# Spectral mixing and routed experts on one core: x read in runs of eight rows, tables and first weights on GpSimd's queue, two batches' copies on ScalarE

## The chip, the cores and the metric

The kernel runs on one core of a Trainium2 chip. The metric is the device time of one execution in microseconds. Before the change it is 1658.18 us, the median of three runs (1657.53 to 1659.67). A profile comes from one further execution of its own.

A core has TensorE (PE, with its weight loads as PEld), VectorE (DVE), ScalarE (ACT), GpSimd (POOL) and SyncE (SP), each with its own stream of instructions in program order. DMAs are issued from the streams of SP, ScalarE and GpSimd (SPq, ACTq and POOLq in the profile) and carried out by 16 DMA engines.

## The reference

```
X = rfft(x, axis=1)                       # x: (8, 2496, 256) float32
y = irfft(X * (filt_r + 1j*filt_i))       # one complex filter for each frequency and channel
x2 = y.reshape(19968, 256)
e = token_ids * 2654435761 % 8            # one of 8 experts for each token
out[e == k] = relu(x2[e == k] @ w1[k]) @ w2[k]     # w1: (8, 256, 1024), w2: (8, 1024, 256)
```

## The kernel before

**The transform.** The sequence length 2496 is split as 39 x 64: position = 64*n1 + n2, with n1 under 39 and n2 under 64. Each of the eight batches passes three stages, all made of float32 matmuls against tables.

- *Stage 1* is a transform over n1. To fill the partitions three values of n2 are stacked: a tile of x has 117 partitions (H = 3 groups of 39), and along its free side HN = 21 columns j of 256 channels. Group h holds n2 = 3j + h. The 64th value, n2 = 63, is left over: it stands as a 22nd column in group 0 alone. `load1` (L171 to L188) reads x in three loads of eight columns (XL), each as one DMA for every group, where a row of 256 channels (1 KB) is followed by the one three positions on; the left-over row has a DMA of its own (L187). `stage1` multiplies by `wf_t`, ScalarE copies the result from PSUM, and ScalarE's queue writes it to a buffer d1 in DRAM (L226), indexed by the place 3j + h.
- *Stage 2* is a transform over n2 with the filter and the way back. `load2` (L228) reads d1 with the 64 places on partitions, as five pieces of four frequencies (tiles t2). `forward` multiplies by `d_t` (L240); VectorE multiplies by the filter in four instructions (L246, L249 twice, L250); `back` (a step later) multiplies by `e_t`, the transposed `d_t` (L262); ScalarE copies (L265) and writes to d2 in DRAM (L269). There are eleven steps for a batch, of which ten have a forward half.
- *Stage 3* is the inverse transform over n1. `load4` (L281) reads d2, `stage3` multiplies by `wi_t`, VectorE copies the result into a tile o (L205, and L200 for the last two columns), beside which it writes each token's number (L287). Then one indirect DMA for each of the 22 columns (L298) scatters the rows to their slots in a buffer xs in DRAM; the slots come from `sidx`. There are two tiles o, and six pieces for a batch.

`products` (L190) is shared by stages 1 and 3 and takes the copying function as an argument.

**The routing.** `count` and `route` count the tokens of each expert and give each token a slot, so that the slots of a tile of 128 belong to one expert; `places` (L467) writes the slots to DRAM and reads them back as `sidx`, in the layout of stage 3. `tile_experts` and `experts` give each tile's expert (`chunk_i`). `blanks` scatters empty rows to unused slots.

**The experts.** A main loop over 163 tiles loads 128 rows of xs (L604), transposes them (`turn`, L612), multiplies by w1 (`up`, L623), applies the relu on ScalarE (L627) and VectorE (L629), multiplies by w2 (`down`, L635), copies (L638) and scatters to the output (L639). Weights are held for two tiles; SP reads an expert's number into a register and loads 1 MB each of w1 and w2 (L322, L324), skipped where the expert stays. The tiles come in four stages: those of a stage hold tokens of the first 2, 4, 6 or 8 batches alone. The two weight buffers serve first as room for x (batch 0 and the first third of batch 1).

**The order.** It is written out by hand. Each piece of work has a time, all are sorted by it, and each engine gets its instructions in that order (L567 to L587). Negative times are the prologue, ahead of the main loop: batches 0 and 1 entirely, batch 2 up to the start of stage 2, the routing and the tables. Pieces with times from 0 on are put into the main loop, one time unit for a tile. `load_tables` (L341) reads one part of `d_t` and of the two filters (four DMAs for these, two of which go backwards by rows); `spread_filters` copies them to the other 64 partitions, on VectorE and ScalarE; `way_back` makes `e_t` from `d_t` on TensorE. Part 0 serves the first four steps of stage 2 and part 1 the rest.

On SP the prologue's order is: x of batch 0; tables part 0; stage 2 input, piece 0 of batch 0; x of batch 1, first third; tables part 1; x, second third; piece 1; x, last third; pieces 2 to 4; `wi_t`; the weights of tiles 0 and 1; then the inputs of batch 1's stage 2, batch 0's stage 3 and x of batch 2, mixed.

Of the kernel before, what the change touches and what calls it, by code (L numbers as in the profile page):

```python
# [12 lines left out]
I32 = mybir.dt.int32  # L13
# [6 lines left out]
P = 128  # L20
# [4 lines left out]

N1, N2 = 39, 64
NS, NQ = N1 // 2 + 1, 64
H, HN = 3, 21  # L30
NR = H * N1
NK = 2 * H * NS
SG = 4
# [29 lines left out]


def dft_tables():
    n1, n2 = np.arange(N1), np.arange(N2)
    s, q = np.arange(NS), np.arange(NQ)
    ph = 2 * np.pi * np.outer(n1, s) / N1
    w = np.stack([np.cos(ph), -np.sin(ph)], 1)
    wf = np.zeros((H, N1, H, 2, NS))  # L70
    wi = np.zeros((H, 2, NS, H, N1))
    v = np.stack([2 * np.cos(ph), -2 * np.sin(ph)], 0)
    v[0, :, 0], v[1, :, 0] = 1.0, 0.0
    for h in range(H):
# [14 lines left out]
    f32 = np.float32  # L89
    return (wf.reshape(NR, NK).astype(f32), wi.reshape(NK, NR).astype(f32),  # L90
            d.reshape(P, NS, P).astype(f32))


def route_table():


    t = np.zeros((P, G + 2 + NQP + HN + 1), np.float32)
    p = np.arange(P)
    n1, j = np.arange(NR) % N1, np.arange(HN)
    t[:NR, G + 2 + NQP:-1] = (N2 * n1 + np.arange(NR) // N1)[:, None] + H * j  # L100
    t[:N1, -1] = N2 * np.arange(N1) + N2 - 1
# [9 lines left out]
def kernel(  # L111
# [38 lines left out]
    dps = pool(ctx, "dps", 1, PSUM)  # L150

    ident = keep.tile([P, P], F32)
    sidx = keep.tile([NR, B, N2], I32)
    tokno = keep.tile([NR, HN + 1], F32)
    chunk_i = keep.tile([1, 2, NT], I32)
    wf_t = cpool.tile([NR, NK], F32)
# [5 lines left out]
    class Batch:  # L162
# [8 lines left out]
        def load1(self, v):  # L171

            k = self.b * NV + v
            if k < 4:
                xt = ws[k // 2][k % 2][0:NR]
                if k % 2 == 0:
                    xt = xt.rearrange("p d (j c) -> p (d j) c", c=C)
            else:
                xt = xpool.tile([NR, XL, C], F32, name=f"x_{self.b}_{v}", tag="x")
            self.x[v] = xt  # L180
            off, n = x.offset + self.b * S * C, min(XL, HN - XL * v)
            for h in range(H):
                nc.sync.dma_start(out=xt[N1 * h:N1 * h + N1, 0:n, :],
                                  in_=bass.AP(tensor=x.tensor, offset=off + (H * XL * v + h) * C,
                                              ap=[[N2 * C, N1], [H * C, n], [1, C]]))
            if n < XL:
                nc.sync.dma_start(out=xt[0:N1, n, :],  # L187
                                  in_=bass.AP(tensor=x.tensor, offset=off + (N2 - 1) * C, ap=[[N2 * C, N1], [1, C]]))  # L188

        def products(self, w, rows, cols, src, dst, copy, u, name):  # L190

# [91 lines left out]
        def stage3(self, u):  # L283

            n = min(XG, HN + 1 - XG * u)
            o = opool.tile([NR, XG, W], F32, name=f"o_{self.b}_{u}", tag="o")
            nc.vector.tensor_scalar(o[:, 0:n, C:].bitcast(I32),  # L287
                                    tokno[:, XG * u:XG * u + n].unsqueeze(2).to_broadcast([NR, n, W - C]),
                                    float(self.b * S), None, op0=OP.add)
            v, half = divmod(u, XL // XG)  # L290
            self.products(wi_t, 2 * NS, N1, self.t4[v][:, half * XG:half * XG + XG, :], o, nc.vector.tensor_copy, u, "pd")
            for i in range(n):
                j = XG * u + i
                r, k = (NR, H * j) if j < HN else (N1, N2 - 1)
                scatter(o[0:r, i, :], sidx[0:r, self.b, k:k + 1], f"xs_{self.b}")

    def scatter(rows, index, group):
        st = nc.gpsimd.indirect_dma_start(  # L298
            out=xs[:], out_offset=bass.IndirectOffsetOnAxis(ap=index, axis=0),
            in_=rows, in_offset=None, bounds_check=NT * TB - 1, oob_is_err=False)  # L300
        for other in ["xs_pad", "xs_read"] + [f"xs_{b}" for b in range(B)]:
            tc.declare_no_dep(st.ins, group=other, reason="distinct rows")
        tc.add_to_no_dep_group(group, st.ins)
# [7 lines left out]
    def weights(i, which):  # L311

        if i >= NT:
            return
        if i >= 2 and which == 0:
            ws[i] = ws[i - 2]
        e = nc.sync.value_load(chunk_i[0:1, 0, i:i + 1], min_val=0, max_val=E - 1)
        kw = {}
        if i >= 2:
            kw = {"cond": nc.sync.value_load(chunk_i[0:1, 1, i:i + 1], min_val=0, max_val=1)}  # L320
        if which == 0:
            nc.sync.dma_start(out=ws[i][0][:], in_=moe_w1[bass.ds(e, 1)].rearrange("one (dp p) f -> p (one dp) f", p=P), **kw)  # L322
        else:
            nc.sync.dma_start(out=ws[i][1][:], in_=moe_w2[bass.ds(e, 1)].rearrange("one (fp p) d -> p (one fp) d", p=P), **kw)  # L324


    rctx = ctx.enter_context(ExitStack())
# [12 lines left out]

    def load_tables(part):  # L341
        sl = S_PARTS[part]
        nc.sync.dma_start(out=d_t[:, sl, :], in_=d_dram.ap()[:, sl, :])
        for k in range(2):
            load_filter(k, sl)

    def load_filter(k, sl):
        filt = (filt_r, filt_i)[k]
        for q in range(2):
            off, step = (0, C) if q == 0 else (N1 * C, -C)  # L350
            nc.sync.dma_start(
                out=f_t[k][32 * q:32 * q + 32, sl, :],
                in_=bass.AP(tensor=filt.tensor, offset=filt.offset + off + sl.start * step,
                            ap=[[N1 * C, 32], [step, sl.stop - sl.start], [1, C]]))
# [112 lines left out]
    def places():  # L467
        slot, slot_i = rv["eid"], rv["eid_i"]
        nc.vector.tensor_reduce(slot[:], rv["acc"][:].rearrange("p e j -> p j e"), axis=AX.X, op=OP.add)
        nc.vector.tensor_copy(slot_i[:], slot[:])  # L470
        nc.gpsimd.dma_start(out=slot_dram[:].rearrange("(p j) -> p j", p=P), in_=slot_i[:])
        for h in range(H):
            n = N2 if h == 0 else H * (HN - 1) + 1
            slots = slot_dram[:]
            nc.gpsimd.dma_start(out=sidx[N1 * h:N1 * h + N1, :, 0:n],
                                in_=bass.AP(tensor=slots.tensor, offset=slots.offset + h,
                                            ap=[[N2, N1], [S, B], [1, n]]))

    def tile_experts():
# [85 lines left out]


    todo = part1(0, spaced(-153, -143, NU)) + [(-152.5, count), (-152.4, route)]  # L567
    todo += [(-152.3, lambda: load_tables(0)), (-141, lambda: load_tables(1))]
    todo += [(t, lambda k=k: way_back(k)) for k, t in enumerate([-142.7, -142.5, -123.5, -123, -122.5])]
    todo += [(-129, lambda: spread_filters(0)), (-122.3, lambda: spread_filters(1)), (-129.5, places)]  # L570
    todo += part2(0, spaced(-128, -90.6, N_2), -142)
    todo += part1(1, spaced(-124, -99, NU), [-141.5, -140.5, -136])
    todo += [(-119, tile_experts), (-113, experts), (-108, blanks)]
    todo += [(-110, lambda: nc.sync.dma_start(out=wi_t[:], in_=wi_dram.ap()))]
    todo += [(-104 + 5 * i, lambda i=i: (weights(i, 0), weights(i, 1))) for i in range(2)]
    todo += part2(1, spaced(-90, -58, N_2), -97) + part3(0, spaced(-81, -48, NU), -90.5)
# [113 lines left out]
```

## Time and profile before

| what | value |
|---|---|
| median of three runs | 1658.18 us |
| profiled execution, its own time | 1654.79 us |
| its span, first to last instruction | 1653.1 us |
| mean granted TensorE clock | 0.963 |
| TensorE busy | 1521.8 us (92%) |
| TensorE weight loads busy | 1380.7 us (84%) |
| VectorE busy | 552.2 us (33%) |
| GpSimd busy | 349.1 us (21%) |
| ScalarE busy | 205.0 us (12%) |
| moved by DMA | 258.28 MB in 172156 packets, mean 156 GB/s |

A window row gives the stretch in us from the start of the span, its length, and for TensorE, its weight loads, VectorE, ScalarE and GpSimd the busy time in us with the count of instructions; then the granted TensorE clock, the DMA share (the mean busy share of the 16 DMA engines) and GB/s moved. A share can come out slightly above 1. A row of the waits gives who waited for whom: us in total, how many times, the longest. A timeline row gives start, duration, engine, line, operation, and count. The first instruction of the main loop's tiles is at 224.06 us.

### The profile page before, as it was taken

To read this page: it belongs to the slowest core of one execution; us is meant where nothing else is said; L and a number is where in the kernel's file an instruction comes from. 1 tells how busy PE (TensorE), PEld (TensorE's weight loads), DVE (VectorE), ACT (ScalarE), POOL (GpSimd) and SP (SyncE) were. 2 spreads that over 40 slices of the span, in tenths; PEclk is the share of its full clock that TensorE was granted. 3 is DMA by queue.
4 is the path that set the end of the run, shared out by engine and by line. 5 is a ranking of instruction groups with operands and counts; after the bars stand their busy time and mean duration, and the time that the engine had idled before them with its cause. 6 is when DMAs were issued, how large, how long until landed. Compare 5 with 4: busy or idle time off the path is not lost.

```text
span 1653.1 us, 26640 instructions
## 1 busy us (share of the span) xinstructions
PE 1521.8 (92%) x9522; PEld 1380.7 (84%) x9522; DVE 552.2 (33%) x1046; ACT 205.0 (12%) x347; POOL 349.1 (21%) x361
## 2 busy tenths in 40 slices
PE   4555669999999999999999999999999999999998
PEld 3434458888888999899989999999899999999997
DVE  6356243353243444324433433222211112121121
ACT  2211102111111111111110111000000000000000
POOL 0015500240331032212221223232211111111111
PEclk7788789999999999999999999999999999999999
DMA  8999666866785796396726844453244312222220
GB/s 205 205 272 265 188 143 173 239 179 161 209 221 156 248 256 163 105 246 149 222 79 186 243 119 145 124 155 116 82 146 138 112 64 92 89 83 90 89 81 12
DMA packets 172156, 258.28 MB, mean 156 GB/s; under 512 B 16297, under 2 KB 141660, under 8 KB 171897
## 3 DMA queue, kind: packets, MB, share of 16 engines
q1 hardware_dynamic: 125057, 170.95, 38.2%
q10 hardware_dynamic: 27608, 42.13, 9.0%
q0 software_dynamic: 19360, 43.50, 8.0%
q8 instruction: 76, 1.25, 0.3%
q14 instruction: 55, 0.45, 0.1%
HBM read 431.38 MB, written 86.09 MB: 313 GB/s over the span
## 4 chain that ended last, share of the span: by engine, by line
PE 43%; issue 37%; POOL 7%; DMA 6%; DVE 4%; SPq 1%; POOLq 1%; ACT 1%; ACTq 0%; DVEq 0%
PE ups L623 15%; PE dps L635 15%; POOL out_dram L639 5%; PE pa L203 4%; PE pd L203 3%; PE pb L240 3%; PE pc L262 3%; DMA t<-d 2%; DVE z L249 2%; POOL xs L298 2%; DMA d<-t 1%; DMA w<-in_x_dram 1%; DMA d<-g 1%; PE xps L612 1%; DVE y L246 1%
## 5 line engine op out<-in xcount | busy, mean ns | idle before, releaser
L623 PEld LDWEIGHTS ups<-xt,w 128*128 128x128 f32 x5216 | 609.5, 192 | 9.7 <-DVE xt L614 1.0
L623 PE MATMUL ups<-xt,w 128*128 128x128 f32 x5216 | 610.5, 275 | 0.6 <-DVE xt L614 0.6
L635 PE MATMUL dps<-w,ht 128*128 128x256 f32 x2608 | 595.9, 382 | 0.0
L635 PEld LDWEIGHTS dps<-w,ht 128*128 128x128 f32 x2608 | 492.5, 192 | 66.6 <-issue 1.6
L639 POOL DMA_INDIRECT out_dram<-osb,xg x163 | 159.9, 981 | 952.9 <-DVE osb L638 903.7
L629 DVE TENSOR_SCALAR ht<-ups 128x512 f32<-128x512 f32 x163 | 112.7, 691 | 535.8 <-PE ups L623 464.8
L298 POOL DMA_INDIRECT xs<-o,sidx x176 | 176.8, 1005 | 260.4 <-DVE o L205 191.8
L627 ACT ACTIVATE ht<-ups 128x512 f32<-128x512 f32 x163 | 97.4, 597 | 1026.4 <-PE ups L623 817.8
L638 DVE COPY osb<-dps 128x256 f32<-128x256 f32 x163 | 69.2, 424 | 405.0 <-PE dps L635 378.1
L240 PE MATMUL pb<-t,d_t 128*128 128x256 f32 x320 | 89.2, 406 | 43.4 <-DMA t<-d 43.4
L249 DVE TENSOR_TENSOR z<-pb,filt 64x512 f32<-64x512 f32 x160 | 110.2, 688 | 2.2
L262 PE MATMUL pc<-y,e_t 128*128 128x256 f32 x320 | 85.9, 392 | 26.6 <-DVE y L250 24.9
L240 PEld LDWEIGHTS pb<-t,d_t 128*128 128x128 f32 x320 | 62.2, 204 | 55.2 <-issue 46.4
L262 PEld LDWEIGHTS pc<-y,e_t 128*128 128x128 f32 x320 | 59.9, 193 | 43.2 <-issue 23.6
L203 PE MATMUL pd<-t,wi_t 120*117 120x256 f32 x320 | 81.9, 401 | 12.2 <-DMA t<-d 8.0
L246 DVE TENSOR_TENSOR y<-pb,filt 128x512 f32<-128x512 f32 x80 | 55.2, 689 | 74.5 <-PE pb L240 67.6
L203 PEld LDWEIGHTS pd<-t,wi_t 120*117 120x117 f32 x320 | 59.1, 191 | 25.1 <-issue 9.5
L265 ACT COPY g<-pc 128x512 f32<-128x512 f32 x80 | 46.9, 586 | 254.3 <-PE pc L262 226.9
L614 DVE COPY xt<-xps 128x256 f32<-128x256 f32 x163 | 67.4, 414 | 5.5 <-PE xps L612 5.5
L612 PE MATMUL xps<-ident,xg 128*128 128x128 f32 x326 | 62.5, 274 | 6.3 <-DMA xg<-xs 6.3
L203 PE MATMUL pa<-x,wf_t 117*120 117x256 f32 x264 | 64.8, 390 | 1.5 <-DVE z L249 1.5
L205 ACT COPY t<-pa 120x512 f32<-120x512 f32 x80 | 46.1, 587 | 123.3 <-PE pa L203 106.8
(93 smaller groups left out, 348.5 us busy)
## 6 DMA issues: line engine op xcount, KB each, us to landing
w<-in_moe_w_dram SPq DMA_DIRECT2D x326, 1024.0 KB
xg<-xs SPq DMA_DIRECT2D x163, 136.0 KB
t<-d SPq DMA_DIRECT2D x80, 256.0 KB
d<-g ACTq DMA_DIRECT2D x80, 256.0 KB
d<-t ACTq DMA_DIRECT2D x16, 960.0 KB
t<-d SPq DMA_DIRECT2D x16, 960.0 KB
x<-in_x_dram SPq DMA_DIRECT2D x39, 312.0 KB
d<-t ACTq DMA_DIRECT2D x8, 600.0 KB
```

Source lines behind the costliest of these rows:

```text
L203: nc.tensor.matmul(out=ps[0:cols * H, k, :], lhsT=w[:], rhs=src[:, 2 * i + k, :], start=True, stop=True)
L240: nc.tensor.matmul(out=ps[:, i, :], lhsT=d_t[:, s, :], rhs=self.t2[s // SG][:, s % SG, :], start=True, stop=True)
L246: nc.vector.tensor_tensor(out=y[:], in0=ps[:], in1=f_t[0][:, sl, :], op=OP.mult)
L249: nc.vector.tensor_tensor(out=z[b], in0=ps[a], in1=f_t[1][a, sl, :], op=OP.mult)
L262: nc.tensor.matmul(out=ps[:, i, :], lhsT=e_t[:, 2 * u + i, :], rhs=pr[:, i, :], start=True, stop=True)
L298: st = nc.gpsimd.indirect_dma_start(out=xs[:], out_offset=bass.IndirectOffsetOnAxis(ap=index, axis=0), in_=rows, in_offset=None, bounds_ch ...
L612: nc.tensor.transpose(out=ps[:, dp, :], in_=xg[i][:, dp * P:(dp + 1) * P], identity=ident[:])
L623: nc.tensor.matmul(out=ps[:, k, :], lhsT=w1[:, dp, fp * P:(fp + 1) * P], rhs=xt[i][:, dp, :], start=(dp == 0), stop=(dp == DP - 1))
L627: nc.scalar.activation(out=dst, in_=ps[:], func=AF.Relu)
L629: nc.vector.tensor_scalar_max(dst, ps[:], 0.0)
L635: nc.tensor.matmul(out=ps[:], lhsT=ht[:, fp, :], rhs=w2[:, fp, :], start=(fp == 0), stop=(fp == FP - 1))
L639: st = nc.gpsimd.indirect_dma_start(out=out[:], out_offset=bass.IndirectOffsetOnAxis(ap=xg[i][:, C:C + 1].bitcast(I32), axis=0), in_=o[:], ...
```

## The change

**x.** Group h now holds 21 neighbouring values of n2: group 1 has 0 to 20, group 2 has 21 to 41 and group 0 has 42 to 63, the left-over one included (`H0`). So eight columns of a partition are eight neighbouring rows of x, 8 KB in a run, and group 0's DMA is one row longer where a batch ends, instead of a DMA of its own. The places in d1 and d2 stay 3j + h; the order of n2 along them is a permutation, which `dft_tables` puts into `d_t`. `sidx` and the token numbers follow: `sidx` holds 22 slots for each partition and batch in place of 64.

**Queues.** The tables (`d_t`, filters) and the weights of tiles 0 and 1 are issued by GpSimd instead of SP. Part 0 of the tables goes first of all pieces; part 1 is issued inside `places`, between the write of the slots and the reads of `sidx`.

**Copies.** Stage 3 of batches 0 and 1 copies from PSUM on ScalarE instead of VectorE. The token numbers (L287) stay on VectorE.

**Times.** The prologue's times are new. On SP the order becomes: x of batch 0; piece 0; x of batch 1, first third; piece 1; x, second and last third; pieces 2 to 4; `wi_t`; and then as before, with the first two loads of x of batch 2 one place earlier each. Stage 1 of batch 1 ends ahead of step 7 of stage 2 of batch 0 (before: ahead of step 8), and `way_back` of part 1 and the spreading of part 1's filters stand around step 3 (before: ahead of step 2). The main loop's times are unchanged.

```diff
+H0 = (2 * HN, 0, HN)
...
 def dft_tables():
-    n1, n2 = np.arange(N1), np.arange(N2)
+    n1 = np.arange(N1)
+    n2 = np.array([H0[i % H] + i // H for i in range(N2)])
...
-    sidx = keep.tile([NR, B, N2], I32)
+    sidx = keep.tile([NR, B, HN + 1], I32)
...
-            off, n = x.offset + self.b * S * C, min(XL, HN - XL * v)
             for h in range(H):
+                n = min(XL, HN + (h == 0) - XL * v)
                 nc.sync.dma_start(out=xt[N1 * h:N1 * h + N1, 0:n, :],
-                                  in_=bass.AP(tensor=x.tensor, offset=off + (H * XL * v + h) * C,
-                                              ap=[[N2 * C, N1], [H * C, n], [1, C]]))
-            if n < XL:
-                nc.sync.dma_start(out=xt[0:N1, n, :],
-                                  in_=bass.AP(tensor=x.tensor, offset=off + (N2 - 1) * C, ap=[[N2 * C, N1], [1, C]]))
+                                  in_=bass.AP(tensor=x.tensor, offset=x.offset + (self.b * S + H0[h] + XL * v) * C,
+                                              ap=[[N2 * C, N1], [C, n], [1, C]]))
...
-            self.products(wi_t, 2 * NS, N1, self.t4[v][:, half * XG:half * XG + XG, :], o, nc.vector.tensor_copy, u, "pd")
+            copy = nc.scalar.copy if self.b < 2 else nc.vector.tensor_copy
+            self.products(wi_t, 2 * NS, N1, self.t4[v][:, half * XG:half * XG + XG, :], o, copy, u, "pd")
...
-                r, k = (NR, H * j) if j < HN else (N1, N2 - 1)
-                scatter(o[0:r, i, :], sidx[0:r, self.b, k:k + 1], f"xs_{self.b}")
+                r = NR if j < HN else N1
+                scatter(o[0:r, i, :], sidx[0:r, self.b, j:j + 1], f"xs_{self.b}")
...
-        e = nc.sync.value_load(chunk_i[0:1, 0, i:i + 1], min_val=0, max_val=E - 1)
-        kw = {}
+        eng, kw = nc.gpsimd if i < 2 else nc.sync, {}
+        e = eng.value_load(chunk_i[0:1, 0, i:i + 1], min_val=0, max_val=E - 1)
...
-            nc.sync.dma_start(out=ws[i][0][:], in_=moe_w1[bass.ds(e, 1)].rearrange("one (dp p) f -> p (one dp) f", p=P), **kw)
+            eng.dma_start(out=ws[i][0][:], in_=moe_w1[bass.ds(e, 1)].rearrange("one (dp p) f -> p (one dp) f", p=P), **kw)
...
-        nc.sync.dma_start(out=d_t[:, sl, :], in_=d_dram.ap()[:, sl, :])
+        nc.gpsimd.dma_start(out=d_t[:, sl, :], in_=d_dram.ap()[:, sl, :])
...
         nc.gpsimd.dma_start(out=slot_dram[:].rearrange("(p j) -> p j", p=P), in_=slot_i[:])
+        load_tables(1)
         for h in range(H):
-            n = N2 if h == 0 else H * (HN - 1) + 1
+            n = HN + (h == 0)
...
-    todo += [(-152.3, lambda: load_tables(0)), (-141, lambda: load_tables(1))]
-    todo += [(t, lambda k=k: way_back(k)) for k, t in enumerate([-142.7, -142.5, -123.5, -123, -122.5])]
-    todo += [(-129, lambda: spread_filters(0)), (-122.3, lambda: spread_filters(1)), (-129.5, places)]
-    todo += part2(0, spaced(-128, -90.6, N_2), -142)
-    todo += part1(1, spaced(-124, -99, NU), [-141.5, -140.5, -136])
-    todo += [(-119, tile_experts), (-113, experts), (-108, blanks)]
+    todo += [(-154, lambda: load_tables(0)), (-129.5, places)]
+    todo += [(t, lambda k=k: way_back(k)) for k, t in enumerate([-142.7, -142.5, -119.5, -119, -118.5])]
+    todo += [(-129, lambda: spread_filters(0)), (-118.3, lambda: spread_filters(1))]
+    todo += part2(0, spaced(-128, -95, N_2), -142)
+    todo += part1(1, spaced(-123.5, -105, NU), [-141.5, -135, -134.5])
+    todo += [(-117, tile_experts), (-113, experts), (-108, blanks)]
     todo += [(-110, lambda: nc.sync.dma_start(out=wi_t[:], in_=wi_dram.ap()))]
-    todo += [(-104 + 5 * i, lambda i=i: (weights(i, 0), weights(i, 1))) for i in range(2)]
-    todo += part2(1, spaced(-90, -58, N_2), -97) + part3(0, spaced(-81, -48, NU), -90.5)
-    todo += part3(1, spaced(-52, -20, NU), -60) + part1(2, spaced(-50, -18, NU), [-75, -70, -40])
+    todo += [(-107 + i, lambda i=i: (weights(i, 0), weights(i, 1))) for i in range(2)]
+    todo += part2(1, spaced(-94, -60, N_2), -103) + part3(0, spaced(-84, -51, NU), -94.5)
+    todo += part3(1, spaced(-54, -21, NU), -62) + part1(2, spaced(-52, -19, NU), [-85, -80, -41])
```

The filters' DMAs and that of w2 change their engine in the same way as those of `d_t` and w1.

More of the change, by code (lines that the diff above doesn't have):

```diff
@@ L98, in route_table @@
     p = np.arange(P)
-    n1, j = np.arange(NR) % N1, np.arange(HN)
-    t[:NR, G + 2 + NQP:-1] = (N2 * n1 + np.arange(NR) // N1)[:, None] + H * j
-    t[:N1, -1] = N2 * np.arange(N1) + N2 - 1
+    r = np.arange(NR)
+    t[:NR, G + 2 + NQP:] = (N2 * (r % N1) + np.array(H0)[r // N1])[:, None] + np.arange(HN + 1)
     for g, b in enumerate(STAGES):
@@ L316, in weights @@
             ws[i] = ws[i - 2]
-        e = nc.sync.value_load(chunk_i[0:1, 0, i:i + 1], min_val=0, max_val=E - 1)
-        kw = {}
+        eng, kw = nc.gpsimd if i < 2 else nc.sync, {}
+        e = eng.value_load(chunk_i[0:1, 0, i:i + 1], min_val=0, max_val=E - 1)
         if i >= 2:
-            kw = {"cond": nc.sync.value_load(chunk_i[0:1, 1, i:i + 1], min_val=0, max_val=1)}
+            kw = {"cond": eng.value_load(chunk_i[0:1, 1, i:i + 1], min_val=0, max_val=1)}
         if which == 0:
-            nc.sync.dma_start(out=ws[i][0][:], in_=moe_w1[bass.ds(e, 1)].rearrange("one (dp p) f -> p (one dp) f", p=P), **kw)
+            eng.dma_start(out=ws[i][0][:], in_=moe_w1[bass.ds(e, 1)].rearrange("one (dp p) f -> p (one dp) f", p=P), **kw)
         else:
-            nc.sync.dma_start(out=ws[i][1][:], in_=moe_w2[bass.ds(e, 1)].rearrange("one (fp p) d -> p (one fp) d", p=P), **kw)
+            eng.dma_start(out=ws[i][1][:], in_=moe_w2[bass.ds(e, 1)].rearrange("one (fp p) d -> p (one fp) d", p=P), **kw)
     rctx = ctx.enter_context(ExitStack())
@@ L350, in load_filter @@
             off, step = (0, C) if q == 0 else (N1 * C, -C)
-            nc.sync.dma_start(
+            nc.gpsimd.dma_start(
                 out=f_t[k][32 * q:32 * q + 32, sl, :],
@@ L471, in places @@
         nc.gpsimd.dma_start(out=slot_dram[:].rearrange("(p j) -> p j", p=P), in_=slot_i[:])
+        load_tables(1)
         for h in range(H):
-            n = N2 if h == 0 else H * (HN - 1) + 1
+            n = HN + (h == 0)
             slots = slot_dram[:]
             nc.gpsimd.dma_start(out=sidx[N1 * h:N1 * h + N1, :, 0:n],
-                                in_=bass.AP(tensor=slots.tensor, offset=slots.offset + h,
+                                in_=bass.AP(tensor=slots.tensor, offset=slots.offset + H0[h],
                                             ap=[[N2, N1], [S, B], [1, n]]))
```

## The prediction

> **What bounds the kernel now.** I read the 40 slices first, then the busy times of stretches, then who waited for whom, then the DMA view.
>
> ```profile
> PE   4555669999999999999999999999999999999998
> DMA  8999666866785796396726844453244312222220
> ```
>
> Each digit is a fortieth of the span, 41.3 us. TensorE is full from the sixth slice on; before that it is half idle while the DMA engines are full. The windows view puts figures to it (busy us per engine, clock, DMA share, GB/s):
>
> ```profile
> 0.00:157.00 157.00, 86.03 (x320) 64.22 (x320) 95.87 (x191) 33.42 (x52) 32.15 (x41) 0.83 0.93 238
> 157.00:225.00 68.00, 34.32 (x110) 24.38 (x110) 17.41 (x32) 7.67 (x14) 25.03 (x26) 0.68 0.78 198
> 225.00:1653.00 1428.00, 1401.43 (x9092) 1292.10 (x9092) 438.91 (x825) 163.95 (x281) 291.95 (x295) 0.99 0.51 145
> ```
>
> From 225 us, where the first expert tile runs, TensorE is busy 1401 of 1428 us, with the same work after the change. Its waits there come to 19.4 us, all on copies by VectorE and ScalarE and none on a DMA. So only the 225 us ahead of it can shrink, the prologue with 120.3 us of TensorE work in it. TensorE's waits in it are:
>
> ```profile
> PE pb L240 <- DMA t<-d: 43.4, 4, 14.3
> PE pc L262 <- DVE y L250: 17.6, 12, 2.3
> PE pa L203 <- DMA w<-in_x_dram: 11.2, 2, 10.1
> PE pd L203 <- DMA t<-d: 8.0, 1, 8.0
> PE xps L612 <- DMA xg<-xs: 6.3, 1, 6.3
> ```
>
> Columns: total us, times, longest. 69 us end on DMAs, 18 us on VectorE's filter product. The four waits for stage 2's input (28.4 to 37.9, 51.7 to 66.0, 102.6 to 112.6, 199.2 to 208.7) are the core of it. The longest is a matter of SP's order:
>
> ```profile
> 35.78 0.68 SPq L343 DMA_DIRECT2D d_t<-d_tbl  x1
> 36.50 1.22 SPq L351 DMA_DIRECT2D filt<-in_filt_r_dram  x2
> 37.76 1.85 SPq L351 DMA_DIRECT2D filt<-in_filt_i_dram  x2
> 40.37 8.85 SPq L183 DMA_DIRECT2D x<-in_x_dram  x3
> 49.26 2.98 SPq L232 DMA_DIRECT2D t<-d  x2
> ```
>
> The second piece of stage 2's input (L232 at 49.26) stands behind the second tables and two loads of x, and takes 14.3 us to land.
>
> **Part by part.** *x in 8 KB runs.* The DMA view of 5 to 10 us, where x is alone, and of 95 to 103 us, with weights and writes (slice lines left out):
>
> ```profile
> DMA packets 867, 0.86 MB, mean 171 GB/s; under 512 B 31, under 2 KB 867, under 8 KB 867
> q1 hardware_dynamic: 867, 0.86, 90.9%
> ...
> DMA packets 1883, 3.22 MB, mean 403 GB/s; under 512 B 135, under 2 KB 1432, under 8 KB 1883
> ```
>
> x in 1 KB packets moves 171 GB/s at a share of 0.91, so 188 GB/s with the engines full; the other stretch moves 403 at 1.05, so 384. The mean of the first 157 us is 238/0.93 = 256. No row has x in 8 KB runs, so its rate lies between 188 (no gain) and 384; I take 256, what the prologue's mixture reaches. Before 157 us x costs 2 x 2.56 + 2 x 0.96 = 7.0 MB: 37.2 us at 188, 27.3 at 256, 18.2 at 384. Gain **10 us** of DMA time (0 to 19). The eight small extra loads (L187, 0.32 us of issue each) also go. The Trainium skill ("DMA: Bandwidth & Descriptors", section "Specifications") gives 512 B as the smallest transfer at line rate. By that rule 1 KB packets have nothing to gain, this term would be 0 and my sum 13 instead of 23; the 171 GB/s beside 403 speak against the rule here.
>
> *Tables on GpSimd's queue.* 1.3 MB of d_t and 2.6 MB of filters leave SP. In 0 to 157 us SP's queue moved 23.14 MB in 63.0% of 157 us, 234 GB/s, and GpSimd's 3.51 MB in 7.3%, 306 GB/s: 3.9 MB take 12.8 us instead of 16.8, **4 us** (0 to 8, the upper end if the 4.2 MB of weights gain as well). On POOL each DMA is one instruction: 1.06 us for the slots, 0.69 for a sidx load of 312 runs, so ten table DMAs cost 7 to 11 us of an engine that is idle from 2.0 to 35.9. The first five go out at 2 us instead of 12 to 26; beside x they can delay the first x (landed at 10.06) or come in its gaps: -2 to +3 us on stage 2's start, which I take at +2. It cannot be more: VectorE's routing chain ends at 35.5 and the filter copy at 36.8, where the first product now starts at 40.0. The second five follow the write of the slots at 36, as on SP now, and stand ahead of the sidx loads; those have to be there by the first scatter (127.2), so their delay of some 5 us is hidden.
>
> *Order on SP.* Stage 2's second input is moved ahead of x's second third, and the tables are out of the way; it should land near 42. Steps two and three of stage 2 then no longer wait for it until 66. What is late next is the second half of the filters: it lands at 58.3 now and ScalarE negates it until 61.0. If that stays, the fifth step (product at 77.7 now) can start at 61: 16.7 us (5 to 22, by how much the tables suffer beside x). The remaining six steps need 6 x 2.77 = 16.6 us of VectorE and 3 us of routing, 20 us where 23.6 are spent: 3 us. The gap of 10.0 us at 102.6 to 112.6 ends on stage 2 input of the second batch, whose write was slowed by 4 MB of weights; after the change its stage 1 ends a step earlier and the weights are issued behind it: 7 us (0 to 10).
>
> *Copies of stage 3 on ScalarE.* For the first batch, interleaved with stage 2 of the second, VectorE is busy 35.5 us of 44 (113 to 157). It loses ten copies of 0.688 us and two of 0.42, 7.7 us, and ScalarE, busy 5.9 of those 44, gets them at 0.587: 7 us (0 to 7.7). If a copy waits on ScalarE for a free o tile (two tiles, 17.3 us of such waits on VectorE's L287 now), the copies of stages 1 and 2 and the writes ScalarE issues stand behind it.
>
> *First weights on POOL.* They stand behind seven scatters of blanks (9 us) and wait for chunk_i; behind them are the scatters of batch 0. They cost four instructions of 1 to 2.3 us (1024 runs at the sidx load's 2.2 ns), hidden by POOL's idle 29 us ahead of 127.2. SP loses 4.4 us of waiting for chunk_i ahead of stage 2's loads; inside the gap above.
>
> **The sum.** The chain of waits would give 16.7 + 3 + 7 + 7 = 34 us by 157 us, but the same 37.4 MB must pass. DMA is busy 0.93 x 157 = 146 us and idle 11; 10 + 4 us less busy leaves 132. With its idle time kept the stretch shrinks by 14, with none left by 25. I take 14 plus half of the idle, **20 us**; the DMA bound thus takes back 14 of the 34. After 157 us the third batch's stage 3 copies are paced by POOL: 22 scatters at 1.295 us are 28.5 of the 30.6 us from 167.9 to 198.5; 1 us at most comes from ScalarE. The last wait, for xg (215.3 to 224), has 0.96 MB of x ahead of it: 5.1 us at 188, 3.7 at 256, some 1.5 us. I take **3 us** for both (-4 to +4). Sum 23 us. The profiled execution took 1654.79 us (span 1653.1), 3.4 below the median of the runs, 1658.18; from the median: **1635 us**.
>
> On the queues the Trainium skill ("DMA: Bandwidth & Descriptors", section "Issuing engines are not separate DMA queues") says that issuing from several engines saves only issue time, as all share 16 DMA engines. By it the table term is 0 instead of 4 and the forecast 1639; the 306 against 234 GB/s above are rates of different packets and do not settle it.
>
> **Rivals.** *x is no faster in long runs.* For it: 12 KB packets of the second tables run beside x in 40 to 52 us, and that stretch reaches only 199 GB/s at 1.07. Then 0 + 4 + 5.5 by 157 us, and 1 behind: 10 us, **1648**. *DMA isn't the bound* and packets only look long because queues interleave: 403 GB/s in one stretch speaks for it, a share over 0.9 from 0 to 157 against it. Then the chain's 34 and 3: **1621**. *Slower: weights ahead of the scatters.* They share POOL's queue, and stage 3 has two o tiles, so the third waits until the weights have landed. If they are issued as late as now (93 us) and get a third of 256 GB/s, 4.2 MB take 49 us and land at 142; then come 42 scatters at 1.295 (54.4), the 6.7 us between batches and the 26.8 from the last scatter to the first tile: 230 instead of 225.3, **1663**. It decides once they land after 137.4; against it speak the earlier stages. *No change*: the main loop gives back what the prologue gains, since its order is fixed; its full TensorE speaks against it: **1658**.
>
> **How the numbers follow.** Forecast 0.46, x no faster 0.18, chain 0.20, no change 0.06, slower 0.10. A measurement of this kernel tells 0.2% (3.3 us) from no change; so faster is 0.84, same 0.06, slower 0.10. The range, 1618 to 1652, spans the second and third cases with their spread and leaves out the last two.
>
> **What would show it.** The first expert tile at about 202 us instead of 225; all later work the same. Packets under 8 KB fall by 17,000 to 20,000 and x's early rate rises over 220 GB/s. The wait of 14.3 us ahead of L240 is gone, and the filter's second half (L359) is what the fifth step waits for. VectorE's share in the overlap falls under 0.75 or the stretch is shorter. Wrong I would be if x stays near 171 GB/s, if the first scatter starts after 125 us, or if TensorE begins to wait for DMAs in the main loop.

## The result and the profile after

The changed kernel takes 1668.83 us (median of four runs, 1668.52 to 1671.55), the kernel before 1658.93 us on the same chip: a ratio of 1.0062, 95% interval 1.0045 to 1.0080. It is 10 us slower where 23 us faster was forecast. The profiled execution took 1668.82 us, its span is 1667.2 us.

The slices of the changed kernel, now 41.7 us each:

```profile
PE   3656559998999999999999999999999999999997
DMA  7988755756786796395726844443244312222220
```

TensorE is full from the sixth or seventh slice on, as before. The DMA row is no longer full ahead of that: 8, 7, 5 and 5 stand where 9, 6, 6 and 6 stood. The same three stretches in the windows view (us, then busy us of TensorE, weight loads, VectorE, ScalarE, GpSimd, then clock, DMA share, GB/s):

```profile
0.00:157.00 157.00, 84.26 (x304) 62.59 (x304) 87.08 (x175) 36.83 (x59) 34.51 (x49) 0.80 0.87 224
157.00:225.00 68.00, 33.54 (x112) 23.00 (x112) 5.81 (x15) 15.34 (x30) 31.09 (x32) 0.75 0.72 194
...
225.00:1667.00 1442.00, 1403.15 (x9106) 1292.36 (x9106) 444.87 (x834) 165.12 (x283) 292.48 (x295) 0.99 0.50 145
```

DMA engines are less busy by 157 us (0.87 for 0.93), as forecast, but they moved less too: 224 GB/s for 238. The saved busy time became idle time, not speed. TensorE's waits ahead of the main loop:

```profile
PE pb L239 <- DMA t<-d: 29.5, 5, 10.0
PE pd L202 <- DMA t<-d: 23.2, 2, 16.0
PE pa L202 <- DMA w<-in_x_dram: 20.8, 3, 13.7
PE pc L261 <- DVE y L249: 13.2, 9, 3.5
PE pd L197 <- issue: 8.6, 2, 5.2
```

The waits for stage 2's input fell from 43.4 to 29.5 us. Those for stage 3's input rose from 8.0 to 23.2, those for x of batch 0 from 11.2 to 20.8. In landmarks of TensorE's timelines (us from the start of the span):

| first matmul of | before | after |
|---|---|---|
| stage 1, batch 0 | 10.1 | 13.7 |
| stage 2, batch 0 | 37.9 | 42.9 |
| its third step (second input) | 66.0 | 60.2 |
| its fifth step | 76.6 | 78.6 |
| stage 2, batch 1 | 112.6 | 104.5 |
| stage 3, batch 0 | 124.7 | 131.5 |
| stage 3, batch 1 | 164.9 | 173.6 |
| first expert tile | 224.1 | 234.7 |

So the loss has two places: 5 us by the start of stage 2, of which 2 are left at its fifth step; and, after 8 us were won by the start of batch 1's stage 2, a swing of 15 us up to stage 3 of batch 0. From there the lead of the kernel before grows from 6.8 to 10.6 us. The rest of the two profiles' 14.1 us lies in the main loop (1429.0 and 1432.5 us). That is within the noise: in the profiles of set 2 below the main loop takes 1428.4 us before the change and 1424.2 after it.

The second place in POOL's and SP's timelines of the changed kernel (start, duration, engine, line, operation):

```profile
104.52 0.98 POOL L299 DMA_INDIRECT xs<-tok,at_i  x1 [0.30 <-issue]
105.48 0.78 POOL L323 DMA_DIRECT2D w<-in_moe_w_dram  x1
106.25 0.95 POOL L325 DMA_DIRECT2D w<-in_moe_w_dram  x1
107.18 0.73 POOL L323 DMA_DIRECT2D w<-in_moe_w_dram  x1
107.88 0.93 POOL L325 DMA_DIRECT2D w<-in_moe_w_dram  x1
134.44 1.06 POOL L299 DMA_INDIRECT xs<-o,sidx  x1 [25.64 <-ACT o L204]
```

and in its chain of waits (start, duration, what):

```profile
114.13 17.21 DMA t<-d
131.34 0.14 issue
131.47 3.73 PE pd L202 x8
```

The weights go out behind the last scatter of blanks, at 105 to 109 us (before: 83 to 93). The first third of stage 3's input, issued at 114.1 by SP, takes 17.2 us to land and TensorE waits 16.0 us for it. The DMA view of 112 to 132 us says with what it shared the engines (queue: packets, MB, share of 16 engines):

```profile
q1 hardware_dynamic: 1528, 1.90, 48.6%
q0 software_dynamic: 904, 3.44, 47.4%
q10 hardware_dynamic: 180, 0.58, 7.2%
```

GpSimd's queue (q0), in which nothing but the weights is left then, moved 3.44 MB, SP's (q1) 1.90. The first four microseconds of it, 114 to 118 us, show how the input fared right after its issue:

```profile
q0 software_dynamic: 379, 1.47, 100.2%
q10 hardware_dynamic: 10, 0.04, 2.5%
q1 hardware_dynamic: 1, 0.00, 0.1%
```

SP's queue moved nothing in them. In 118 to 122 us it moved 0.24 MB beside 0.89 MB of weights, and only from 122 us on, as the weights ran out, the bulk of what it had to move.

### The profile page after: what moved, and what is told of

Its sections match the earlier page's. It is cut to its first block, busy times and chain, and to the rows that moved or that the text cites. A ratio compares the mean times of both kernels' runs of the same rounds, so it can differ in the third digit from the quotient of the medians.

```text
span 1667.2 us, 26682 instructions
## 1 busy us (share of the span) xinstructions
PE 1521.0 (91%) x9522; PEld 1377.9 (83%) x9522; DVE 537.8 (32%) x1022; ACT 217.3 (13%) x371; POOL 358.1 (21%) x375
## 4 chain that ended last, share of the span: by engine, by line
PE 49%; issue 32%; DMA 9%; POOL 5%; DVE 3%; ACT 1%; SPq 1%; POOLq 0%; another core or an unknown queue 0%; ACTq 0%; DVEq 0%
PE ups L625 18%; PE dps L637 18%; POOL out_dram L641 4%; PE pd L202 3%; DMA t<-d 3%; PE pa L202 3%; PE pb L239 2%; PE pc L261 2%; DMA d<-t 2%; DMA d<-g 1%; POOL xs L299 1%; PE xps L614 1%; DVE z L248 1%; DMA w<-in_x_dram 1%; DMA xg<-xs 1%
## 5 line engine op out<-in xcount | busy, mean ns | idle before, releaser
L239 PE MATMUL pb<-t,d_t 128*128 128x256 f32 x320 | 90.6, 411 | 29.9 <-DMA t<-d 29.5
L202 PE MATMUL pd<-t,wi_t 120*117 120x256 f32 x320 | 82.0, 402 | 23.8 <-DMA t<-d 23.2
L202 PEld LDWEIGHTS pa<-x,wf_t 117*120 117x120 f32 x264 | 47.7, 186 | 15.0 <-ACT t L204 3.6
```

The costliest lines, as they stand in the source:

```text
L202: nc.tensor.matmul(out=ps[0:cols * H, k, :], lhsT=w[:], rhs=src[:, 2 * i + k, :], start=True, stop=True)
L239: nc.tensor.matmul(out=ps[:, i, :], lhsT=d_t[:, s, :], rhs=self.t2[s // SG][:, s % SG, :], start=True, stop=True)
```

## The experiments

Each set ran on one chip, with runs of the kernel before beside it; the sets ran on four chips (4 and 5 on one), and the kernel before took 1646 to 1657 us there. Ratios are to the kernel before of the same set, with 95% intervals. Runs of one kernel differ by 5 to 16 us within a set, so a single profile shows where a wait stands, and the ratio what it costs.

**Set 1: one part of the change undone.** The first weights on SP at their old times:

```diff
-        eng, kw = nc.gpsimd if i < 2 else nc.sync, {}
-        e = eng.value_load(chunk_i[0:1, 0, i:i + 1], min_val=0, max_val=E - 1)
+        e = nc.sync.value_load(chunk_i[0:1, 0, i:i + 1], min_val=0, max_val=E - 1)
+        kw = {}
...
-    todo += [(-107 + i, lambda i=i: (weights(i, 0), weights(i, 1))) for i in range(2)]
+    todo += [(-104 + 5 * i, lambda i=i: (weights(i, 0), weights(i, 1))) for i in range(2)]
```

> The changed kernel with the first weights issued by SP again, at their old times. Theory 'the weights collide': in the changed kernel GpSimd issues them at 105.5 to 108.8 us, behind the blanks, and their 4.2 MB share the DMA engines with batch 0's stage 3 input, for which TensorE waits 16.0 us until 131.5. On SP they go out once chunk_i is there (87 us in the changed kernel), so that wait falls under 6 us and the time falls by 8 to 11 us, to 1658 to 1661. Rival 'tables crowd x': the loss comes from the first 38 us, so 1667 to 1669 stays.

Measured 1.0057 (1.0035 to 1.0078).

Part 0 of the tables on SP, behind x of batch 0 (part 1 stays on GpSimd; the filters' DMAs follow `teng` as well):

```diff
-        nc.gpsimd.dma_start(out=d_t[:, sl, :], in_=d_dram.ap()[:, sl, :])
+        teng = nc.sync if part == 0 else nc.gpsimd
+        teng.dma_start(out=d_t[:, sl, :], in_=d_dram.ap()[:, sl, :])
...
-    todo += [(-154, lambda: load_tables(0)), (-129.5, places)]
+    todo += [(-152.3, lambda: load_tables(0)), (-129.5, places)]
```

> The changed kernel with part 0 of the tables on SP again, behind the x of batch 0 (part 1 stays on GpSimd). Rival 'tables crowd x': x's first third lands at 10 us instead of 13.7 and stage 2 starts at 38 instead of 42.9; if that carries through, the time falls by 5 us to 1664. Theory 'the weights collide': the early 5 us are absorbed further on (stage 2 of batch 0 ended only 2 us later than before the change), so the time falls by 0 to 2 us, 1667 to 1669.

Measured 1.0052 (1.0031 to 1.0074).

Stage 3's copies on VectorE:

```diff
-            copy = nc.scalar.copy if self.b < 2 else nc.vector.tensor_copy
+            copy = nc.vector.tensor_copy
```

> The changed kernel with stage 3's copies of batches 0 and 1 on VectorE again. Theory 'the weights collide': the copies were never what stage 3 waited for, because from 131 us on stage 3 is paced by GpSimd's scatters; 1667 to 1671. Rival 'ScalarE is the new bottleneck': copies waiting for a free o tile hold up those of stages 1 and 2 behind them on ScalarE (3.2 and 2.3 us of such waits in the changed kernel's last 40 us); undone, the time falls by 3 to 6 us, 1663 to 1666. If the copies were worth the 7 us that the prediction gave them, it rises to 1675.

Measured 1.0086 (1.0058 to 1.0114).

x in 1 KB runs again (the parts of the diff that touch n2, `sidx` and `load1` undone):

> The changed kernel with x read in 1 KB runs again (old grouping of n2, with the left-over row's own DMA), all else changed. Theory 'x is no faster in long runs': 13 to 14 GB/s for each DMA engine in the changed kernel's packets of x as against 12 to 13 in the old ones, so the time stays within 3 us of 1668.8. If the packing does what the prediction took (10 us of DMA time), the time rises by 5 to 10 us to 1674 to 1679. If long packets hold up the others' short ones, it falls by 3 us or more.

Measured 1.0096 (1.0064 to 1.0128).

The expectations were in us of another chip, and the set had no run of the changed kernel itself. That kernel has 1.0062 (1.0045 to 1.0080) in the result above and 1.0081 (1.0050 to 1.0112) in set 2, and all four intervals here overlap both. So no part taken back alone is shown to return anything. The theory that the weights on SP give back the whole loss is refuted: in that run's profile the waits for stage 3's input are down to 7.7 us from 23.2, and the time is still 1.0057. Nor does part 0 of the tables alone carry it.

**Set 2: the changed kernel as reference, and single parts put into the kernel before.**

> The changed kernel as it is, on the chip of this set, as the reference for its parts. All theories: 1.004 to 1.010 of the time before; TensorE's wait for batch 0's stage 3 input at 12 us or more.

> The kernel before as it is, for its profile on the chip of this set: ratio 0.998 to 1.002; first expert tile 8 to 12 us earlier than in the changed kernel's profile.

Measured 1.0081 (1.0050 to 1.0112) and 1.0010 (0.9987 to 1.0033). The first expert tile starts at 228.4 and 218.0 us in their profiles, and TensorE waits 12.2 us at the longest for stage 3's input.

The weights alone moved to GpSimd (the four lines of `weights` in the change's diff, at the old times):

> The kernel before with only the first weights moved to GpSimd, at their old times. They stand behind the seven scatters of blanks there (88 to 98 us) and go out at about 98 to 102 instead of 83 to 93. Theory 'the weights collide': they meet the inputs of batch 1's stage 2 and of batch 0's stage 3; slower by 4 to 10 us (1.0025 to 1.006). Rival 'tables crowd x': no effect of the weights, within 2 us (0.999 to 1.001).

Measured 1.0083 (1.0053 to 1.0112): this part alone costs as much as the whole change. Its POOL timeline:

```profile
100.37 0.97 POOL L298 DMA_INDIRECT xs<-tok,at_i  x1 [0.30 <-issue]
101.33 0.78 POOL L322 DMA_DIRECT2D w<-in_moe_w_dram  x1
102.10 0.97 POOL L324 DMA_DIRECT2D w<-in_moe_w_dram  x1
103.04 0.73 POOL L322 DMA_DIRECT2D w<-in_moe_w_dram  x1
103.73 0.93 POOL L324 DMA_DIRECT2D w<-in_moe_w_dram  x1
```

SP issued the same four at 83 to 87 us in the kernel before on this chip. TensorE waits for stage 3's input twice, 16.5 us in total, instead of once for 8.4. The write ahead of batch 0's input takes 10.6 us here, and the first third of that input 16.7 us to land.

The grouping of n2 alone (x in 8 KB runs):

> The kernel before with only the new grouping of n2, so that x is read in runs of 8 KB, at the old times. Prediction: 10 us of DMA time less, so 5 to 10 us faster (0.994 to 0.997). Theory 'x is no faster in long runs': within 3 us (0.998 to 1.002), with x alone (5 to 10 us) near 190 GB/s instead of 171.

Measured 1.0015 (0.9999 to 1.0031). The DMA view of 5 to 10 us, first of the kernel before, then with x packed, both of this set:

```profile
DMA packets 916, 0.90 MB, mean 180 GB/s; under 512 B 37, under 2 KB 916, under 8 KB 916
...
q1 hardware_dynamic: 916, 0.90, 91.8%
```

```profile
DMA packets 153, 0.94 MB, mean 188 GB/s; under 512 B 38, under 2 KB 38, under 8 KB 38
...
q1 hardware_dynamic: 153, 0.94, 83.3%
```

With a sixth of the packets the engines are shown less busy, and x moves at 188 GB/s instead of 180: the first matmul starts at 9.5 us with x packed and at 9.6 without. The share fell by 8 points; the rate rose by 4%.

**Set 3: why the weights cost, and the other two parts alone.** The weights on GpSimd (the same lines of `weights`), ahead of the blanks:

```diff
-    todo += [(-104 + 5 * i, lambda i=i: (weights(i, 0), weights(i, 1))) for i in range(2)]
+    todo += [(-108.5 + .1 * i, lambda i=i: (weights(i, 0), weights(i, 1))) for i in range(2)]
```

> The kernel before with the first weights on GpSimd's queue, but ahead of the blanks instead of behind them, so that they are issued about when chunk_i is there (82 to 87 us), as early as on SP. Theory 'they are late' (behind the blanks, at 101 to 105 us, they meet the stage inputs): back to 0.998 to 1.003. Rival 'the queue itself' (on GpSimd's queue they no longer stand in line ahead of stage 2's input but take a share beside it): as slow as behind the blanks, 1.006 to 1.010.

Measured 1.0023 (1.0007 to 1.0040). POOL issues them like this:

```profile
85.32 0.74 POOL L322 DMA_DIRECT2D w<-in_moe_w_dram  x1 [40.95 <-DMA d<-t]
87.18 0.92 POOL L324 DMA_DIRECT2D w<-in_moe_w_dram  x1 [1.12 <-PE pb L240]
89.41 0.70 POOL L322 DMA_DIRECT2D w<-in_moe_w_dram  x1 [1.31 <-DMA d<-t]
91.27 0.90 POOL L324 DMA_DIRECT2D w<-in_moe_w_dram  x1 [1.16 <-PE pa L203]
92.16 0.33 POOL L519 MEMSET tok<- 128x256 int32 x1
```

The same queue, twelve to sixteen us earlier, and most of the loss is gone: it is their place behind the blanks that costs, more than the queue. What is left, 0.2%, can't be told from the tables' or the packing's.

The weights on SP, but behind the last x of batch 2:

```diff
-    todo += [(-104 + 5 * i, lambda i=i: (weights(i, 0), weights(i, 1))) for i in range(2)]
+    todo += [(-39.5 + .5 * i, lambda i=i: (weights(i, 0), weights(i, 1))) for i in range(2)]
```

> The kernel before with the first weights still on SP, but issued behind the last x of batch 2 (about 176 us), where the DMA share is 0.70 and GpSimd paces stage 3; they are needed at 224. Theory 'the weights collide with the stage inputs': the gap at 102 to 112 us shrinks to 6 us or less and the time falls by 4 to 8 us, 0.995 to 0.9975. Rival 'the collision is only GpSimd's': 0.999 to 1.001. If the weights then hold up stage 2's input of batch 2 behind them: up to 1.004.

Measured 1.0009 (0.9992 to 1.0027): no gain. In its profile stage 2 of batch 1 starts at 106.9 us (109.9 in the profile of the kernel before of set 2), and stage 3 of batch 1 at 159.7 (162.2), but that stage's matmuls then spread over some 36 us instead of 28, while the weights pass. The first expert tile starts at 224.3 us (218.0).

The tables alone on GpSimd (`d_t` and filters, part 1 issued inside `places` as in the change):

```diff
-    todo += [(-152.3, lambda: load_tables(0)), (-141, lambda: load_tables(1))]
+    todo += [(-154, lambda: load_tables(0))]
```

> The kernel before with only the tables moved to GpSimd (part 0 first of all, part 1 between the slots and sidx), at the old times. Theory 'tables crowd x': the first matmul starts at 12 to 14 us instead of 9.6 to 10.1 and stage 2 at 41 to 43 instead of 38 to 39; 1.001 to 1.003. Prediction: stage 2's second input lands near 42 to 50 instead of 66 and the time falls by 5 us or more, 0.997 or less.

Measured 1.0016 (1.0002 to 1.0030). TensorE's waits:

```profile
PE pb L240 <- DMA t<-d: 33.3, 4, 10.4
PE pc L262 <- DVE y L250: 17.9, 12, 2.3
PE pa L203 <- DMA w<-in_x_dram: 16.8, 1, 16.8
PE pd L203 <- DMA t<-d: 9.3, 1, 9.3
...
PE pe L365 <- DMA d_t<-d_tbl: 6.2, 1, 6.2
```

The wait for x goes up to 16.8 us, more than expected, and a wait of 6.2 us for part 1 of `d_t` is new (0.2 and 0.8 us in the two profiles of the kernel before). The waits for stage 2's input go down by 10, and the sum is about even.

The copies alone on ScalarE (one line in `stage3`):

> The kernel before with only the copies of stage 3 of batches 0 and 1 on ScalarE. Prediction: 7 us of VectorE's work leave the chain between 113 and 157 us: 0.995 to 0.998. Theory 'that stretch is bound by DMA and by GpSimd's scatters': within 2 us, 0.999 to 1.001. Rival 'ScalarE becomes the bottleneck': 1.002 to 1.005.

Measured 1.0007 (0.9990 to 1.0023).

**Set 4: do the losses add up, and do the tiles o matter?** Weights and part 0 of the tables both on SP again, in the changed kernel:

> The changed kernel with both the first weights and part 0 of the tables on SP again; part 1 on GpSimd, packed x, copies on ScalarE and the new times stay. If the weights and the early tables are separate losses, their undoing adds up: 1.001 to 1.004 (each alone left 1.0057 and 1.0052 where the changed kernel has 1.008). If a common rest remains (new times, copies): 1.004 to 1.007.

Measured 1.0005 (0.9990 to 1.0020): the whole loss is gone, with packed x, part 1 of the tables on GpSimd, the copies on ScalarE and the other new times still in. Each of the two parts alone left a loss of half a per cent in set 1, and the intervals there lie clear of this one: with either part in place most of the loss is there, and without both it is gone. The same profile shows what may stand in the way of a gain (VectorE, who waited for what: total, times, longest):

```profile
DVE y L245 <- PE pb L239: 60.2, 11, 15.4
DVE o L286 <- DMA xs<-o,sidx: 47.0, 9, 10.9
```

These are 47 us of waits for scatters to land and free a tile o.

Only the new times, in the kernel before:

> The kernel before with only the new times of the prologue; tables and weights on SP at their old times. Theory 'the new order costs the rest': 1.003 to 1.006. Rival 'the new order is neutral or good by itself': 0.996 to 1.001, with stage 2's second input landing before 60 us instead of 66.

Measured 1.0049 (1.0030 to 1.0068). So the new times cost by themselves what they do not cost beside packed x, part 1 of the tables on GpSimd and the copies on ScalarE. Which of these makes up for it was not separated.

The kernel before with tiles o of two columns, four of them:

```diff
-    opool = pool(ctx, "op", 2)
+    opool = pool(ctx, "op", 4)
...
-            o = opool.tile([NR, XG, W], F32, name=f"o_{self.b}_{u}", tag="o")
+                o = opool.tile([NR, 2, W], F32, name=f"o_{self.b}_{u}_{i}", tag="o")
```

> The kernel before with each tile o of stage 3 split into two tiles of two columns (four instead of two, in the same space), so that a piece waits for the landing of two scatters instead of four. Theory 'stage 3 turns slow scatters into TensorE's waits through the two tiles o' (25.4 us of such waits on VectorE in the profile of the kernel before on this chip): 3 to 6 us faster, 0.996 to 0.998. Rival 'GpSimd's 1.295 us for each scatter sets the pace anyway': 0.999 to 1.001.

Measured 0.9968 (0.9955 to 0.9982). VectorE's long waits on scatters (25.4 us on L287 in set 2's profile of the kernel before) are not among those of this profile:

```profile
DVE y L246 <- PE pb L240: 49.7, 9, 14.8
DVE o L302 <- PE pd L297: 19.4, 6, 9.5
```

Its copies (L302) wait for TensorE instead. This is 4 to 5 us faster than the kernel before, and the lowest ratio of all runs. Whether the gain lies in the prologue or also in the main loop, where the tiles are split too, was not separated.

The same with the late weights:

> The kernel before with the split tiles o and the first weights on SP behind the last x of batch 2. The late weights alone gave 1.0009: stage 2 of batch 1 started 3 us earlier, and stage 3 of batch 1 took 36 us instead of 28. Theory 'slow scatters through the tiles o': with smaller tiles the late weights' gain comes through, 0.993 to 0.997. Rival: the 4.2 MB cost the same wherever they stand; as p_halves, within 2 us.

Measured 0.9976 (0.9956 to 0.9996), no better than the split alone: the late weights bring nothing here either.

**Set 5: the split in the changed kernel.** With weights and part 0 of the tables on SP:

> The changed kernel with the first weights and part 0 of the tables on SP again (1.0005 by itself) and with split tiles o (0.9968 in the kernel before). In the profile without the split VectorE waits 47 us for scatters to land on L286. Theory 'slow scatters through the tiles o': the split gains at least as much as in the kernel before, 0.993 to 0.997. Rival 'the split's gain was tied to the old order': 0.998 to 1.001.

Measured 1.0004 (0.9983 to 1.0025): the gain does not carry over, as the rival had it. The waits did not go away here, though: VectorE still waits 31.2 us for scatters (47.0 without the split), so whether these waits hold this kernel back stays open.

The changed kernel with the split alone:

> The changed kernel with split tiles o and nothing else. Theory 'the weights cost through stage 3's input' (TensorE's wait of 12 to 16 us for L280, ahead of any scatter): the split returns only what it returns in the kernel before, 0.3%, so 1.003 to 1.006. Rival 'the change loses through the tiles o': all of the loss goes, 0.997 to 1.001.

Measured 1.0053 (1.0029 to 1.0078). Its interval overlaps that of the changed kernel (1.0050 to 1.0112), and most of the loss stays: it does not go through the tiles o in the main.

**All twenty profiles side by side.** TensorE's waits for stage 3's input ahead of 240 us come to 16.5 to 23.3 us in the seven kernels' profiles with the weights behind the blanks on GpSimd, and to 6.1 to 11.3 us in the other thirteen. The first matmul starts at 11.6 to 18.3 us in the seven with part 0 of the tables first on GpSimd, and at 9.5 to 10.8 us in the other thirteen. Both effects of the change on the waits are thus shown beyond the noise of single profiles. How a wait becomes time is less direct, as sets 1 and 4 show.

## Why the prediction was wrong

**What bounds the kernel** was read rightly: the main loop did not change beyond 3.5 us, and the difference is made ahead of it, by waits on DMAs (70 to 74 us of TensorE's waits on x and on the inputs of stages 2 and 3 in the profiles of the changed kernel, 61 to 63 before).

**First weights on POOL, costed at nothing: the step that failed.** The prediction priced their four instructions on POOL (1 to 2.3 us each; they took 0.73 to 0.95) and hid them in POOL's idle time. It gave no price to the 4.2 MB behind them, and even counted their leaving ahead of batch 1's stage 2 as part of a gain. On POOL, past seven scatters of blanks, they are issued 19 to 23 us later, at 105.5 to 107.9 us instead of 83.0 to 89.2, out of a stretch in which stage 2 of batch 0 works from tiles it already has, into one in which TensorE waits for batch 0's stage 3 input. The wait for that input is 16.0 us in the changed kernel; the weights alone give the full loss (1.0083), and ahead of the blanks 1.0023. The slower rival named this queue and these weights, with 0.10; but it let the scatters' tile wait for them, which set 5 speaks against, and it set the point of decision at a landing after 137 us. The weights had landed by the first scatter at 134.4 us (GpSimd's queue moved 0.01 MB in 126 to 132 us), and the loss was there.

**The start, "it cannot be more".** The range of -2 to +3 bounded the gain, by VectorE's routing chain, and only guessed the loss. Measured: the first matmul 3.6 us later and stage 2 5.0 us later. With the tables alone x's first third came at 16.8 us. Part 0 of the tables, 1.6 MB, then stands beside x instead of behind it, and x is what everything starts with. How much time this costs depends on the rest: the tables alone give 1.0016, the changed kernel with the weights on SP and the tables still early 1.0057, with both back on SP 1.0005.

**x in 8 KB runs, 10 us (0 to 19).** The measured term is 0, the lower end: 1.0015 alone. The step that failed is the division of a rate by a DMA share. 171 GB/s at a share of 0.91 was read as 188 at full share with room up to 384, but the share of x fell with longer packets while the rate stayed (180 to 188 GB/s). The first rival had this, with 0.18. The Trainium skill ("DMA: Bandwidth & Descriptors", section "Specifications") gives 512 B as the smallest transfer at line rate, by which 1 KB packets have nothing to gain from packing. The prediction weighed the rule and went with 171 beside 403 GB/s; 1.0015 agrees with the rule. What holds x near 190 GB/s with either packet was not tried and stays open. Longer packets did show in one place: beside the early tables on GpSimd's queue the first matmul starts at 16.8 and 18.3 us with x in 1 KB packets (`p_tables_pool`, `u_x_1k`) and at 11.6 to 13.7 us in the five profiles with 8 KB packets. No gain in time came of it that the ratios show.

**Tables, 4 us of DMA time, and SP's order, 16.7 us.** In 38 to 66 us, where the tables' second part, x of batch 1 and stage 2's input pass, the kernel before moves 5.28 MB at 189 GB/s, the changed one 5.48 MB at 196, though GpSimd's queue now carries 2.34 MB of it:

```profile
DMA packets 1149, 5.48 MB, mean 196 GB/s; under 512 B 237, under 2 KB 259, under 8 KB 852
...
q1 hardware_dynamic: 656, 3.11, 50.9%
q0 software_dynamic: 489, 2.34, 39.5%
```

So the queues shared one rate. The Trainium skill ("DMA: Bandwidth & Descriptors", section "Issuing engines are not separate DMA queues") says that they run on the same 16 engines and interleave; 189 and 196 GB/s agree. The second input, put ahead of x's second third, was to land near 42 us. It was issued at 40.75 and landed at 60.1 (18.9 us instead of 14.3, with the tables beside it); the step was 5.8 us earlier, not 24, and the fifth step 2.0 us later instead of 16.7 us earlier. The fifth step waited 6.0 us for a piece of stage 2's input, not for the filters that the prediction named. SP's queue in the changed kernel:

```profile
38.13 1.15 SPq L231 DMA_DIRECT2D t<-d  x2
39.33 1.38 SPq L185 DMA_DIRECT2D w<-in_x_dram  x3
40.75 1.13 SPq L231 DMA_DIRECT2D t<-d  x2
41.92 21.96 SPq L185 DMA_DIRECT2D x<-in_x_dram  x6
```

**The gap ahead of batch 1's stage 2, 7 us (0 to 10)**: right in place, and 8.1 us earlier at its end. But it was spent at once: the stretch behind it needs stage 3's input, and the weights, now later, are beside it.

**Copies on ScalarE, 7 us (0 to 7.7).** VectorE was busy 35.5 of 44 us in that stretch, and the chain ran through it, but a copy moved is not a wait removed. Measured alone 1.0007 (0.9990 to 1.0023), undone 1.0086 where the changed kernel has 1.0062 and 1.0081: nothing that can be told from zero. In the profile with the copies alone moved, ScalarE waits 16.3 us for scatters to free a tile o, and TensorE 11.8 us for ScalarE's copies, where it waited 6.1 us for VectorE's in set 2's kernel before. The prediction had named this wait and given it no price.

**The last wait, 3 us (-4 to +4).** From stage 3 of batch 1 to the first expert tile it takes 61.1 us instead of 59.2, 2 us the other way.

**The sum.** The parts were put together under a bound on DMA busy time, with half of the idle time used up. That was the wrong budget: DMA idle time grew (a share of 0.87 instead of 0.93 by 157 us). Each stage ends on a round trip through DRAM, and by the landmarks what was saved in one place was waited for in the next. By the experiments no part of the change is a gain by itself. The weights are a loss alone (1.0083), the new times are (1.0049), the tables hardly (1.0016). These do not add up: in the changed kernel, weights and part 0 of the tables taken back one at a time leave some 0.5% each, and together nothing. Why the parts overlap like this was not separated.

## What to carry to other kernels

When a DMA is moved to another queue, price its bytes in the stretch where they will now pass, and ask which wait of that stretch they stand beside; the issuing instruction is the small part. A full DMA share is no rate: divide bytes by it only where the profile shows a faster stretch of the same kind of transfer. When a hand-written order is tuned, times that cost nothing beside one set of other edits can cost half a per cent without them.

## What was not expected of the hardware

x read in packets of 8 KB instead of 1 KB went at 188 GB/s instead of 180, with a share of the DMA engines of 0.83 instead of 0.92. A later stretch of the kernel before, 95 to 103 us with weights, writes and blanks, went at 403 GB/s.

With 2.7 MB of weights still to pass on GpSimd's queue, a load issued by SP moved nothing for some 4 us and took 17.2 us to land. The same queue order went with a long wait for stage 3's input (16.5 to 23.3 us) in every profile that had it.

From chip to chip the kernel before took 1646 to 1659 us, a spread as large as the change's effect of 10 to 13 us; on one chip its runs spread by up to 16 us. Its first expert tile started at 224.1 us in one profile and at 218.0 in another.
